# Four edits to the schedule of a Fourier mixing and maxout kernel: the order of the head, three split units, and when a copy is made

## The chip, the cores and the metric

The kernel runs on one core of a Trainium2 chip. The core has five instruction queues that run side by side: TensorE (PE in the profile; PEld is its loading of weights), VectorE (DVE), ScalarE (ACT), GpSimd (POOL) and SyncE (SP, which here only issues transfers). DVE, ACT and PE can read or write PSUM, where products are summed; POOL works in SBUF alone. Each engine takes its instructions strictly in the order in which the kernel wrote them, and waits at semaphores for the others. The metric is the time of one execution on the device in microseconds (us); lower is better.

## The reference

The input x is 8 batches of 3072 rows by 256 columns. Each batch goes through a Fourier transform over its rows and one over its columns, and the real part is kept. The result, 24576 rows of 256, then goes through a maxout layer with a width of 768:

```python
X = np.fft.fft(np.fft.fft(x, axis=1), axis=2).real
h = np.maximum(np.maximum(X @ w1, X @ w2), X @ w3)
out = h @ w_out
```

## The kernel before, in words

**Mixing.** The transform over rows is done in two stages of products with small tables, and its even and odd parts are kept apart in two bf16 tiles per batch, `tE` and `tO` (128 x 1536 each, class `Mix`). The transform over columns is never carried out on x: it is folded into the weights once, at the start (`products`, `keep`, `differ`, `prep_first`, `prep_second`; the results are `g_all`, `gd_all`, `gw`). Because sine and cosine are symmetric, the lower 64 partitions of x's tile `xt` are loaded, and the upper 64 are a mirrored copy of them: `mirror` (L129, and L133 for the first column) in batches 0 and 1, and from batch 2 on eight pieces (`turn`, L129 on ACT) and `mirror_first` (L138 on ACT). `xt` has two buffers, for even and odd batches.

**Units.** A batch has 18 units (3 blocks of 512 columns times 6 groups of 128 hidden features); g counts them over all batches. A unit makes the maximum of three products for a row (`hp`) and for its mirror row (`hm`). `begin` makes the first half and `finish` the second; the loop at the end writes begin(g), then finish(g-1). There are two forms:

- Not split (`unit_plus`, `unit_minus`, `unit_out`): the weights are taken relative to w1, so two sums remain, `pse2` and `pse3`. Four products of 512 columns make the first half (L484, L485) and two more (L491) turn it into the second; each half is taken by a Relu on ACT (`stmp`, L497) and a maximum on DVE (L498).
- Split (`third` and the branches in `begin` and `finish`): the third product is made apart and earlier, two units ahead. TensorE makes `e3` and `d3` (L856, L858), ACT scales `d3` into `odd3` (L860), DVE adds a rank-one term into `even3` (L861), and POOL makes their sum and difference (`plus3`, `minus3`, L865). Then `begin` needs two products (L875, L876) and one DVE instruction (L877), and `finish` one product (L491) and one DVE instruction (L889). A split unit has five products of 512 columns, another six.

`is_split` decides: odd units from g = 7 on are split; even ones by their place in the batch, in no unit of batch 0 and in the units 0, 4, 8, 12 and 14 of all others (`EXTRA`, `EXTRA_LAST`, which are the same).

**Second layer.** The products with `w_out` of one block of columns (L547, with L563 and L570) are pieces of a generator. `l2_some(10)` issues ten of them after each unit, so that TensorE has work while DVE, ACT and POOL finish a unit. DVE adds the linear part (L575), and the rows are stored by SP, or scattered by POOL (L651, `scatter`, units 0, 4, 8, 14 by `PACE`, and unit 16 in the last batch). The last block of the last batch has a form of its own (`l2_last`).

**Order.** The order is written out by hand, no scheduler changes it. `at(batch, unit, fn)` puts a function into a plan that is run after a unit's products: loads of a later batch's x (`load_x`, on POOL's queue, in units 13 and 18 three batches ahead), its mirrored copies (`turn`), and the mixing of the next batch (`ahead0`, `ahead`).

**Head.** Before unit 0 the mixing of batch 0 is done in a straight line: x comes in four pieces, each is mirrored by DVE, multiplied (`m.s`, L394), and evicted to `tb`; DVE transposes `tb` (L427); `k_first` (L696) makes the first 512 columns of `tE` and `tO`, in two halves of 256 each, evicted by DVE and ACT (L698). The fourth piece's first column is copied by POOL (L133). Three DVE instructions of one column (L220) make `sgn` and `dif`, after the transpose. PSUM has eight banks: in the head five belong to `ps_s` and three to `ps_f`; then `ps_s` is given up and its banks go to `ps_l1`, `ps_w3` and `ps_o`, in which the units sum.

Of the kernel before, what the change touches and what calls it, by code (L numbers as in the profile page):

```python
# [9 lines left out]
FP32 = mybir.dt.float32  # L10
# [4 lines left out]
ALU = mybir.AluOpType  # L15
# [13 lines left out]

FIRST_OF = (4, 8, 1)  # L30
PACE = (0, 4, 8, 14)
EXTRA, EXTRA_LAST = (0, 4, 8, 12, 14), (0, 4, 8, 12, 14)


def _parts(g):

    done = [(12 + i - 1, slice(128 * i + 96, 128 * i + 128)) for i in range(4)]
    for i in range(4 if g < 2 else 3):
        done.append((FIRST_OF[g] + i - 1, slice(128 * i, 128 * i + 96)))
    if g == 2:  # L40
        done += [(16, slice(384, 480, 2)), (15, slice(385, 480, 2))]
    return done
# [3 lines left out]
def kernel(  # L46
# [9 lines left out]
    nc = tc.nc  # L56

    B, S, D = x.shape
# [3 lines left out]
    TOKB = 512  # L62
    NHALF = 1536
    UNITS = 3 * NJC
# [8 lines left out]
    ps_f = ctx.enter_context(tc.tile_pool(name="ps_f", bufs=3, space=bass.MemoryType.PSUM))  # L73
# [30 lines left out]
    g_all = consts.tile([128, 4 * DFF], BF16, tag="g_all")  # L104
    g_all = g_all.rearrange("p (c k j) -> p c k j", k=4, j=128)
# [6 lines left out]
    sgn = consts.tile([128, 1], FP32, tag="sgn")  # L112
    wcol = consts.tile([128, NJC], FP32, tag="wcol")
    dif = consts.tile([128, 1], FP32, tag="dif")
    t_mid = consts.tile([128, 2, B], BF16, tag="t_mid")

    def load_x(b, s0, s1, h):

        rows = x[b].rearrange("(a s) d -> a s d", s=96)
        lo, hi = (s0, s1) if h == 0 else (max(s0, 1), min(s1, 48))  # L120
        src = rows[:, lo:hi, :] if h == 0 else rows[:, 97 - hi:97 - lo, :][:, ::-1, :]
        return nc.gpsimd.dma_start(out=xt[b % 2][32 * h:32 * h + 32, lo:hi, :], in_=src)  # L122

    def mirror(b, s0, s1):

        t = xt[b % 2]
        fn = (nc.vector.tensor_copy, (nc.gpsimd.tensor_copy, nc.vector.tensor_copy)[s0 >= 25],
              nc.scalar.copy)[min(b, 2)]
        fn(out=t[64:128, s0:s1, 1:128], in_=t[0:64, s0:s1, 255:128:-1])  # L129
        if b < 2:  # L130
            if b == 0:
                fn = nc.scalar.copy if s0 < 40 else nc.gpsimd.tensor_copy
            fn(out=t[64:128, s0:s1, 0], in_=t[0:64, s0:s1, 128])  # L133

    def mirror_first(b):

        t = xt[b % 2]
        nc.scalar.copy(out=t[64:128, :, 0], in_=t[0:64, :, 128])  # L138
# [3 lines left out]
    ps_s = ps_s_cm.__enter__()  # L142
# [7 lines left out]
    pidx = gen.tile([128, 1], FP32, tag="pidx")  # L150
# [56 lines left out]
    turn = gen.tile([128, 2], FP32, tag="turn")  # L207
# [10 lines left out]
    def scal(out, in0, s1, op0, s2=None, op1=None, eng=None):  # L218
        kw = {} if op1 is None else {"op1": op1}
        return (eng or nc.vector).tensor_scalar(out=out, in0=in0, scalar1=s1, scalar2=s2,  # L220
                                                op0=op0, **kw)
# [113 lines left out]
    def prep_first():  # L335

        for i in range(2):
            for half in range(2):
                psg = ps_f.tile([128, 512], FP32, name="psg", tag="ps")
                product(psg, 0, i, half, 384, 768)  # L340
                (nc.vector.tensor_copy, nc.scalar.copy)[half](
                    out=g_all[:, 3:6, 2 * i + half, :],
                    in_=psg[:, 0:384].rearrange("p (c j) -> p c j", j=128))
                if half:
                    differ(i, i + 1, 384, 768)
                yield
# [8 lines left out]
    def prep_second():  # L355

        for jp in range(NJC // 2):
            pst = ps_f.tile([128, 512], FP32, name="pst", tag="ps")
            for k in range(2):
                jc = jp * 2 + k  # L360
                for fc in range(2):
                    nc.tensor.matmul(
                        pst[:, k * 256:(k + 1) * 256],
                        w1_bf[:, fc * DFF + jc * 128: fc * DFF + jc * 128 + 128],
                        md[fc], start=(fc == 0), stop=(fc == 1))
            (nc.scalar.copy if jp == 2 else nc.vector.tensor_copy)(
                out=g1t[:, jp * 512:(jp + 1) * 512], in_=pst)
            yield
        psw = ps_f.tile([128, 512], FP32, name="psw", tag="ps")
        for half in range(2):  # L370
            for jc in range(NJC):
                nc.tensor.matmul(
                    psw[:, half * 256:(half + 1) * 256],
                    g1t[:, jc * 256 + half * 128: jc * 256 + half * 128 + 128],
                    wout_bf[:, jc * 256:(jc + 1) * 256],
                    start=(jc == 0), stop=(jc == NJC - 1))
        nc.vector.tensor_copy(out=gw[:, 0:512], in_=psw)
        nc.scalar.activation(out=gw[:, 512:768], in_=psw[:, 256:512], func=AX.Copy, scale=sgn)
        yield
# [96 lines left out]
                                 tab[:, NHALF:NHALF + 1], start=True, stop=True)  # L476
            nc.scalar.copy(out=t_mid[:, :, self.b], in_=ps3[:, 0:2])

    def unit_plus(te, to, jc, n, pool3, tag3):

        pse2 = ps_l1.tile([128, TOKB], FP32, name="pse2", tag="pse2")
        pse3 = pool3.tile([128, TOKB], FP32, name="pse3", tag=tag3)
        for (pse, i) in ((pse2, 0), (pse3, 1)):
            nc.tensor.matmul(pse[:, 0:n], g_all[:, jc, 2 * i, :], te, start=True, stop=False)  # L484
            nc.tensor.matmul(pse[:, 0:n], g_all[:, jc, 2 * i + 1, :], to, start=False, stop=True)  # L485
        return pse2, pse3

    def unit_minus(pses, to, jc):
# [177 lines left out]
    def warm_up(n):  # L666
        for _ in range(n):
            nc.tensor.matmul(warm, zero[:, 0:128], zero, start=True, stop=True)
# [10 lines left out]
    m.s(2, pool=ps_s)  # L679
    m.s(3, pool=ps_s)  # L680
    warm_up(1)
    mirror(0, *FIRST[3])
    m.s(4, pool=ps_s)
    warm_up(2)
# [4 lines left out]
    def k_first(which):  # L689

        for h in range(2):
            ps2 = ps_s.tile([128, 512], FP32, name="ps2", tag="ps")
            for (i, cols) in _parts(0):
                at = cols.start - 256 * h
                if 0 <= at < 256:
                    nc.tensor.matmul(ps2[:, at:at + cols.stop - cols.start], m.col(i, which),  # L696
                                     (te_tab, to_tab)[which][:, cols], start=True, stop=True)
            (dve, nc.scalar.copy)[h](out=(m.tE, m.tO)[which][:, 256 * h:256 * h + 256],  # L698
                                     in_=ps2[:, 0:256])

    m.s(6, pool=ps_s)
    m.t()
    scal(sgn, pidx, 0.0, ALU.is_equal)
    scal(sgn, sgn, 2.0, ALU.mult, -1.0, ALU.add)
    scal(dif, sgn, 1.0, ALU.subtract)
    warm_up(2)
    nc.scalar.activation(out=nmd_all, in_=vm, func=AX.Sin, scale=float(-2.0 * math.pi / 256.0),
                         bias=turn[:, 1:2])
# [46 lines left out]
    ps_w3 = ctx.enter_context(tc.tile_pool(name="ps_w3", bufs=1, space=bass.MemoryType.PSUM))  # L755
    ps_o = ctx.enter_context(tc.tile_pool(name="ps_o", bufs=2, space=bass.MemoryType.PSUM))
# [3 lines left out]
    first, second = prep_first(), prep_second()  # L760
# [10 lines left out]
    def at(b, unit, fn):  # L771
        plan.setdefault((b + unit // UNITS, unit % UNITS), []).append(fn)
# [27 lines left out]
    def turn(b, ch):  # L800
        mirror(b, *EIGHTHS[ch])
# [16 lines left out]
    for b in range(2, B):  # L818
        for h in range(2):
            if b > 2:  # L820
                at(b - 3, (13, 18)[h], lambda b=b, h=h: load_x(b, 0, NS, h))
        for ch in range(8):
            at(b - 2, 5 + ch + 3 * (b == 2), lambda b=b, ch=ch: turn(b, ch))
        at(b - 2, 13 + 3 * (b == 2), lambda b=b: mirror_first(b))

    ahead0 = {3: ("s0", "s1"), 4: ("s2", "y0"), 5: ("s3", "s4"), 6: ("s5", "s6", "y1", "u"),
              7: ("z0", "z1"), 12: ("x",), 13: ("kO0",), 14: ("v0", "kE0", "kO1"),
# [10 lines left out]

    def is_split(g):
        if g % 2 == 0:  # L840
            return (UNITS <= g < B * UNITS and
                    g % UNITS in (EXTRA if g < (B - 1) * UNITS else EXTRA_LAST))
        return 7 <= g < B * UNITS

    def operands(g):
# [21 lines left out]
    def begin(g, dst):  # L867

        te, to, _, jc = operands(g)
        if is_split(g):  # L870
            if g % 2:
                pse2 = ps_l1.tile([128, TOKB], FP32, name="pse2", tag="pse2")
            else:
                pse2 = ps_w3.tile([128, TOKB], FP32, name="pse3", tag="pse3")
            nc.tensor.matmul(pse2, g_all[:, jc, 0, :], te, start=True, stop=False)  # L875
            nc.tensor.matmul(pse2, g_all[:, jc, 1, :], to, start=False, stop=True)  # L876
            nc.vector.scalar_tensor_tensor(out=dst, in0=pse2, scalar=0.0, in1=sums[g][0],  # L877
                                           op0=ALU.max, op1=ALU.max)
            return (pse2,)
        pses = unit_plus(te, to, jc, TOKB, *((ps_o, "po") if g % 2 else (ps_w3, "pse3")))  # L880
        unit_out(pses, dst, TOKB)
        return pses

# [11 lines left out]
    for g in range(B * UNITS):  # L895
        b, u = divmod(g, UNITS)
        blk, jc = divmod(u, NJC)
# [14 lines left out]
        pses = begin(g, hp[:, jc, :])  # L912
# [53 lines left out]
```

## Time and profile before

| | before |
|---|---|
| median of 3 runs (lowest to highest) | 388.24 us (387.73 to 388.91) |
| the profiled execution, its own time | 388.26 us |
| its span in the profile | 386.5 us |
| busy in the span: PE, DVE, POOL, ACT | 369.5, 335.7, 331.7, 242.7 us |
| granted TensorE clock | 1.00 |

Mean durations of the instructions that the change touches, all 128x512:

| line | engine | what | ns |
|---|---|---|---|
| L865 | POOL | plus, minus | 1269, 1270 |
| L860 | ACT | odd | 597 |
| L861 | DVE | even | 737 |
| L877, L889 | DVE | hp, hm of a split unit | 687, 680 |
| L497 | ACT | stmp of a unit that is not split | 599 |
| L498 | DVE | hp, hm of a unit that is not split | 687 |
| L129 | ACT | one copy of x of 64x762 | 820 to 825 |

A profile is read in three steps. The busy times say which engine could be the bound. The chain that ended last says which instruction waited for which, back from the end. The order of time shows, for one stretch, each instruction with its start, its duration and, in brackets, how long its engine had stood still and what ended that. A matmul's duration contains its latency, so the distance between two starts is what TensorE really spends on it.

### The profile page before, as it was taken

What the parts mean: (1) busy time and instruction counts of PE and PEld (TensorE: products, weight loads), DVE (VectorE), ACT (ScalarE), POOL (GpSimd) and SP (SyncE); (2) the same over time, 40 slices, a digit from 0 to 9 for tenths busy, and PEclk for the clock granted to TensorE, in tenths of its full rate; (3) what the DMA queues carried; (4) which work ended last, traced back from release to release, by engine and by line L of the source; (5) the groups of instructions that cost most, each with busy time, mean ns of one, the idle gap of its engine ahead of it and who ended that gap; (6) DMA issues with size and microseconds to landing.
All of it is one profiled execution on the core that took longest, in us unless ns stands there. A gap on an engine that the chain in (4) does not pass through costs nothing.

```text
span 386.5 us, 7957 instructions
## 1 busy us (share of the span) xinstructions
PE 369.5 (96%) x2737; PEld 234.8 (61%) x2786; DVE 335.7 (87%) x566; ACT 242.7 (63%) x455; POOL 331.7 (86%) x355
## 2 busy tenths in 40 slices
PE   6699999999999999999999999999999999999994
PEld 2354566565665666656665666666665667666664
DVE  7798797789997998989987998989987998989982
ACT  6877789567756677567756777567856436434320
POOL 9994557968999899989999899989988899879991
PEclk9999999999999999999999999999999999999999
DMA  8999736695269735695269834695224633312217
GB/s 118 168 197 152 158 114 101 189 162 177 71 133 204 196 120 106 181 213 180 67 120 200 209 110 112 188 187 184 85 56 128 186 113 97 96 61 98 77 63 225
DMA packets 51299, 54.13 MB, mean 140 GB/s; under 512 B 25813, under 2 KB 44268, under 8 KB 50563
## 3 DMA queue, kind: packets, MB, share of 16 engines
q0 software_dynamic: 19392, 26.45, 33.3%
q1 hardware_dynamic: 31334, 26.57, 26.5%
q10 hardware_dynamic: 532, 0.59, 0.5%
q8 instruction: 22, 0.36, 0.4%
q14 instruction: 19, 0.16, 0.1%
HBM read 36.95 MB, written 30.81 MB: 175 GB/s over the span
## 4 chain that ended last, share of the span: by engine, by line
PE 81%; POOL 9%; DVE 4%; issue 3%; ACT 2%; DVEq 0%; POOLq 0%
PE po L547 29%; PE pse L491 9%; PE pse L876 5%; PE e L856 5%; PE d L858 5%; PE pse L875 5%; PE po L570 4%; PE pse L485 4%; PE pse L484 3%; PE ps L460 3%; POOL plus L865 3%; PE ps L394 3%; PE pl L563 2%; POOL minus L865 2%; POOL xt L122 1%
## 5 line engine op out<-in xcount | busy, mean ns | idle before, releaser
L865 POOL TENSOR_TENSOR plus<-even,odd 128x512 bf16<-128x512 f32 x104 | 132.0, 1269 | 38.5 <-DVE even L861 31.1
L865 POOL TENSOR_TENSOR minus<-even,odd 128x512 bf16<-128x512 f32 x104 | 132.1, 1270 | 0.0
L860 ACT ACTIVATE odd<-d 128x512 f32<-128x512 f32 x104 | 62.1, 597 | 63.8 <-PE d L858 50.3
L877 DVE SCALAR_TENSOR_TENSOR hp<-pse,plus 128x512 bf16<-128x512 f32 x104 | 71.4, 687 | 26.0 <-PE pse L876 21.5
L547 PE MATMUL po<-wout_bf,hp 128*128 128x256 bf16 x576 | 86.1, 273 | 0.0
L547 PE MATMUL po<-wout_bf,hm 128*128 128x256 bf16 x576 | 78.6, 273 | 0.0
L861 DVE SCALAR_TENSOR_TENSOR even<-vb,wcol,e 128x512 f32<-128x512 bf16 x104 | 76.6, 737 | 0.0
L547 PEld LDWEIGHTS <-hp 128*128 128x128 bf16 x576 | 56.3, 98 | 26.2
L889 DVE SCALAR_TENSOR_TENSOR hm<-pse,minus 128x512 bf16<-128x512 f32 x104 | 70.7, 680 | 0.8 <-PE pse L485 0.4
L547 PEld LDWEIGHTS <-hm 128*128 128x128 bf16 x576 | 56.3, 98 | 16.3
L491 PE MATMUL pse<-tO,gd_all 128*128 128x512 bf16 x183 | 63.2, 380 | 0.8 <-DVE hp L877 0.2
L497 ACT ACTIVATE stmp<-pse 128x512 bf16<-128x512 f32 x80 | 47.5, 599 | 19.0 <-PE pse L491 8.8
L129 ACT COPY xt<-xt 64x762 bf16<-64x762 bf16 (+1 forms) x48 | 39.8, 838 | 2.3 <-DMA xt<-in_x_dram 1.3
L575 DVE TENSOR_TENSOR kq<-po,even 128x512 f32<-128x512 f32 x60 | 40.9, 682 | 0.0
L856 PE MATMUL e<-tE,g_all 128*128 128x512 bf16 x104 | 39.4, 379 | 0.3
L858 PE MATMUL d<-tO,gd_all 128*128 128x512 bf16 x104 | 39.4, 379 | 0.0
L876 PE MATMUL pse<-tO,g_all 128*128 128x512 bf16 x94 | 35.6, 379 | 1.7 <-issue 1.0
L570 PE MATMUL po<-gw,tO 128*128 128x512 bf16 x92 | 34.9, 379 | 0.0
L498 DVE TENSOR_TENSOR hp<-pse,stmp 128x512 bf16<-128x512 f32 x40 | 27.5, 687 | 6.7 <-ACT stmp L497 3.6
L875 PE MATMUL pse<-tE,g_all 128*128 128x512 bf16 x84 | 31.9, 380 | 0.7 <-DVE hm L498 0.5
L567 ACT COPY even<-pl 128x512 f32<-128x512 f32 x46 | 26.8, 583 | 8.3 <-DVE kq L575 7.8
L498 DVE TENSOR_TENSOR hm<-pse,stmp 128x512 bf16<-128x512 f32 x40 | 27.5, 687 | 4.2 <-ACT stmp L497 3.0
(183 smaller groups left out, 485.4 us busy)
## 6 DMA issues: line engine op xcount, KB each, us to landing
db<-tb SPq DMA_DIRECT2D x21, 192.0 KB
xt<-in_x_dram POOLq DMA_DIRECT2D x5, 784.0 KB, 8.2
xt<-in_x_dram POOLq DMA_DIRECT2D x5, 752.0 KB, 8.7
out_dram<-obuf SPq DMA_DIRECT2D x8, 384.0 KB
out_dram<-kq SPq DMA_DIRECT2D x8, 384.0 KB
vb<-vd SPq DMA_DIRECT2D x23, 128.0 KB
out_dram<-kq SPq DMA_DIRECT2D x7, 288.0 KB
out_dram<-kq SPq DMA_DIRECT2D x15, 128.0 KB
```

Of the source, the lines that this page charges most:

```text
L491: nc.tensor.matmul(pse, gd_all[:, jc, i, :], to, start=False, stop=True, skip_group_check=True)
L498: nc.vector.tensor_tensor(out=dst, in0=src3, in1=stmp[:, 0:n], op=ALU.max)
L547: nc.tensor.matmul(po, hcols(jc), wout_bf[:, jc * 256:(jc + 1) * 256], start=False, stop=(jc == NJC - 1), skip_group_check=True)
L856: nc.tensor.matmul(e3, g_all[:, jc, 2, :], te, start=True, stop=True)
L858: nc.tensor.matmul(d3, gd_all[:, jc, 1, :], to, start=True, stop=True)
L860: nc.scalar.activation(out=odd3, in_=d3, func=AX.Copy, scale=-0.5)
L861: nc.vector.scalar_tensor_tensor(out=even3, in0=vb, scalar=wcol[:, jc:jc + 1], in1=e3, op0=ALU.mult, op1=ALU.add)
L865: nc.gpsimd.tensor_tensor(out=dst, in0=even3, in1=odd3, op=op)
L875: nc.tensor.matmul(pse2, g_all[:, jc, 0, :], te, start=True, stop=False)
L876: nc.tensor.matmul(pse2, g_all[:, jc, 1, :], to, start=False, stop=True)
L877: nc.vector.scalar_tensor_tensor(out=dst, in0=pse2, scalar=0.0, in1=sums[g][0], op0=ALU.max, op1=ALU.max)
L889: nc.vector.scalar_tensor_tensor(out=dst, in0=pses[0], scalar=0.0, in1=sums.pop(g)[1], op0=ALU.max, op1=ALU.max)
```

## The change

It has four parts.

1. In the head, the first column of the fourth piece of batch 0's x is copied by DVE, directly behind its mirror, and not by POOL; `sgn` and `dif` are made before that mirror; `k_first` takes its PSUM tiles for `tO` from `ps_f`; and unit 0 multiplies `tE` into both sums before it multiplies `tO`.
2. In batch 1, the eight copies of batch 3's x and the copy of its first column are placed in the units 6 to 13 and 14, and not 5 to 12 and 13.
3. In batch 0, the units 12 and 14 are split.
4. In the last batch, unit 14 is not split.

```diff
-EXTRA, EXTRA_LAST = (0, 4, 8, 12, 14), (0, 4, 8, 12, 14)
+EXTRA = (12, 14), (0, 4, 8, 12, 14), (0, 4, 8, 12)
...
             if b == 0:
-                fn = nc.scalar.copy if s0 < 40 else nc.gpsimd.tensor_copy
+                fn = nc.scalar.copy if s0 < 40 else nc.vector.tensor_copy
             fn(out=t[64:128, s0:s1, 0], in_=t[0:64, s0:s1, 128])
...
-    def unit_plus(te, to, jc, n, pool3, tag3):
+    def unit_plus(te, to, jc, n, pool3, tag3, first=False):
 
         pse2 = ps_l1.tile([128, TOKB], FP32, name="pse2", tag="pse2")
         pse3 = pool3.tile([128, TOKB], FP32, name="pse3", tag=tag3)
-        for (pse, i) in ((pse2, 0), (pse3, 1)):
-            nc.tensor.matmul(pse[:, 0:n], g_all[:, jc, 2 * i, :], te, start=True, stop=False)
-            nc.tensor.matmul(pse[:, 0:n], g_all[:, jc, 2 * i + 1, :], to, start=False, stop=True)
+        steps = [(pse2, 0, 0), (pse2, 0, 1), (pse3, 1, 0), (pse3, 1, 1)]
+        if first:
+            steps = steps[0::2] + steps[1::2]
+        for (pse, i, k) in steps:
+            nc.tensor.matmul(pse[:, 0:n], g_all[:, jc, 2 * i + k, :], (te, to)[k],
+                             start=(k == 0), stop=(k == 1))
         return pse2, pse3
...
     warm_up(1)
+    scal(sgn, pidx, 0.0, ALU.is_equal)
+    scal(sgn, sgn, 2.0, ALU.mult, -1.0, ALU.add)
+    scal(dif, sgn, 1.0, ALU.subtract)
     mirror(0, *FIRST[3])
...
-            ps2 = ps_s.tile([128, 512], FP32, name="ps2", tag="ps")
+            ps2 = (ps_s, ps_f)[which].tile([128, 512], FP32, name="ps2", tag="ps")
...
     m.t()
-    scal(sgn, pidx, 0.0, ALU.is_equal)
-    scal(sgn, sgn, 2.0, ALU.mult, -1.0, ALU.add)
-    scal(dif, sgn, 1.0, ALU.subtract)
     warm_up(2)
...
         for ch in range(8):
-            at(b - 2, 5 + ch + 3 * (b == 2), lambda b=b, ch=ch: turn(b, ch))
-        at(b - 2, 13 + 3 * (b == 2), lambda b=b: mirror_first(b))
+            at(b - 2, 5 + ch + 3 * (b == 2) + (b == 3), lambda b=b, ch=ch: turn(b, ch))
+        at(b - 2, 13 + 3 * (b == 2) + (b == 3), lambda b=b: mirror_first(b))
...
     def is_split(g):
         if g % 2 == 0:
-            return (UNITS <= g < B * UNITS and
-                    g % UNITS in (EXTRA if g < (B - 1) * UNITS else EXTRA_LAST))
+            return g < B * UNITS and g % UNITS in EXTRA[(g >= UNITS) + (g >= (B - 1) * UNITS)]
         return 7 <= g < B * UNITS
...
-        pses = unit_plus(te, to, jc, TOKB, *((ps_o, "po") if g % 2 else (ps_w3, "pse3")))
+        pses = unit_plus(te, to, jc, TOKB, *((ps_o, "po") if g % 2 else (ps_w3, "pse3")),
+                         first=(g == 0))
```

## The prediction

> **What bounds the kernel now.** I read the page's busy shares, then the chain that ended last, then the order of time around every place where that chain leaves TensorE or TensorE starts late.
>
> ```profile
> PE 369.5 (96%) x2737; PEld 234.8 (61%) x2786; DVE 335.7 (87%) x566; ACT 242.7 (63%) x455; POOL 331.7 (86%) x355
> ...
> PE 81%; POOL 9%; DVE 4%; issue 3%; ACT 2%; DVEq 0%; POOLq 0%
> ```
>
> TensorE is the bound; what counts is its work and the moments at which it starts late. At full rate 512-column products start 0.216 us apart (20.62, 20.84, 21.05) and 256-column ones 0.108, so a larger step between two starts is lost time. After 20 us I find four losses that the change touches.
>
> Order of time, head (start, duration, engine, line, operands, in brackets the idle time before and who ended it):
>
> ```profile
> 14.04 0.22 POOL L133 COPY xt<-xt 64x9 bf16<-64x9 bf16 x1
> 14.31 0.41 PE L394 MATMUL ps<-xt,tab 128*64 128x512 bf16 x2 [0.74 <-POOL xt L133]
> 15.55 3.77 DVE L427 STREAM_TRANSPOSE yb<-tb 128x2048 uint32<-128x2048 uint32 x1
> 19.86 0.37 ACT L698 CAST tE<-ps 128x256 bf16<-128x256 f32 x1 [0.19 <-PE ps L696]
> 20.20 0.37 ACT L698 CAST tO<-ps 128x256 bf16<-128x256 f32 x1
> 20.62 0.38 PE L484 MATMUL pse<-tE,g_all 128*128 128x512 bf16 x1 [0.46 <-ACT tO L698]
> ```
>
> TensorE's first stage waits for POOL's column copy; its first unit multiplies tE, but waits for tO. Batch 1, units 5 to 7:
>
> ```profile
> 84.82 0.82 ACT L129 COPY xt<-xt 64x762 bf16<-64x762 bf16 x1 [1.32 <-DMA xt<-in_x_dram]
> 87.26 0.82 ACT L129 COPY xt<-xt 64x762 bf16<-64x762 bf16 x1
> 88.11 0.60 ACT L497 ACTIVATE stmp<-pse 128x512 bf16<-128x512 f32 x1
> 88.74 0.69 DVE L498 TENSOR_TENSOR hm<-pse,stmp 128x512 bf16<-128x512 f32 x1 [0.49 <-ACT stmp L497]
> 89.48 0.38 PE L875 MATMUL pse<-tE,g_all 128*128 128x512 bf16 x1 [0.54 <-DVE hm L498]
> ```
>
> ACT stands at the first copy of batch 3's x until the load lands; stmp, hm and TensorE follow late. Last batch:
>
> ```profile
> 367.69 1.28 POOL L865 TENSOR_TENSOR plus<-even,odd 128x512 bf16<-128x512 f32 x1
> 369.01 0.69 DVE L877 SCALAR_TENSOR_TENSOR hp<-pse,plus 128x512 bf16<-128x512 f32 x1 [1.16 <-POOL plus L865]
> 369.75 0.38 PE L491 MATMUL pse<-tO,gd_all 128*128 128x512 bf16 x1 [0.25 <-DVE hp L877]
> ```
>
> From 347.9 POOL has no gap worth naming; at unit 15 DVE, then TensorE, wait for it.
>
> **The change, part by part.**
>
> *Column on DVE.* DVE's mirror (13.36, 0.65) ends at 14.01. The nearest row, DVE's L133 of 64x12, takes 0.18 and starts 0.07 before its predecessor ends: done at 14.12, TensorE at 14.17, a gain of 0.14. Ends: 0.06 as in the shortest DVE rows (gain 0.25), or held by a POOL instruction (below). Everything up to the transpose hangs on this product (L401 at 14.76, transpose at 15.55), so the 0.14 goes on. POOL loses 0.22 of work; the weight loads, x0u copies, x loads and yb copies queued behind start up to 0.18 earlier. The three sgn/dif instructions (3 x 0.15) move into DVE's 0.84 idle before 13.36, which ends on a load: nothing; without that gap 0.45 on the same path.
>
> *Products with tE first.* They now need only ACT's tE, ending at 20.23 instead of tO's 20.57; tO's two PSUM tiles come from the other pool, so the unit's banks don't wait for tO either. Start 20.28 for 20.62: 0.34. The third product, at 20.71, finds tO ready (20.57 + 0.05). The first sum of the unit ends only 0.13 earlier, so hp follows at about 22.5, but its reader starts at 23.43 - 0.48 = 22.95: covered by 0.45. From 20.62 to 28.6 TensorE starts are dense, and its small waits at 29 to 46 follow ACT and DVE work that TensorE itself started. Head: 0.14 + 0.34 = **0.48** (from 0, all absorbed there, to 0.59).
>
> *Units 12 and 14 of batch 0 split.* Six products become five: 2 x 0.216 = **0.43** less TensorE. ACT loses 2 x 599 and gains 597 ns per unit. DVE: 737 + 687 + 680 for 2 x 687, +0.73 each; POOL: +2.54 each. The gaps before:
>
> ```profile
> 53.45 1.27 POOL L865 TENSOR_TENSOR plus<-even,odd 128x512 bf16<-128x512 f32 x1 [2.05 <-DVE even L861]
> 55.79 0.69 DVE L877 SCALAR_TENSOR_TENSOR hp<-pse,plus 128x512 bf16<-128x512 f32 x1 [0.69 <-PE pse L876]
> 58.09 1.27 POOL L865 TENSOR_TENSOR plus<-even,odd 128x512 bf16<-128x512 f32 x1 [2.14 <-ACT xt L129]
> 61.16 0.69 DVE L877 SCALAR_TENSOR_TENSOR hp<-pse,plus 128x512 bf16<-128x512 f32 x1 [1.24 <-PE pse L876]
> ```
>
> POOL idles 2.05 + 2.14 here and 0.31 + 0.88 + 0.69 up to 66.67, in all 6.07 for 5.08; DVE 1.93 for 1.46. Queued behind on POOL are unit 13's and 15's sums, batch 3's first load (60.52) and a scatter (61.43). Placing the sums one after another from 51.45, unit 15's end at 61.4, so that load leaves 0.9 late; its second half, which decides, is issued at 72.82 after the gaps. Batch 1's units 11 to 15 run the same order of instructions with no late TensorE start but one of 0.09 at 98.61: I take no new wait. Ends: 0.43 gained, or DVE's 1.46 all exposed (1.03 lost).
>
> *Batch 3's copies a unit later.* The first copy moves behind unit 6's first stmp, odd and even, to where the second stands now (87.26, some 86.5 without the stall); the load landed at 84.75. The stall goes: 89.48 against 88.56 + 2 x 0.108 = 88.78, 0.70, plus 0.07 at 87.05: **0.77** (ends 0 and 0.77). Late next is the last copy and the first-column copy at units 13 and 14; behind them on ACT stand the evictions at 103.69 and 104.17, 0.93 later at most, with 1.21 of ACT idle following: nothing. No DMA moves with them.
>
> *Unit 14 of the last batch not split.* TensorE +0.216, ACT +0.6, DVE -0.73, POOL -2.54. Unit 15's plus ends 2.5 earlier, so three late starts go: 369.75 against 368.68 + 6 x 0.108 = 369.33 (0.42); 371.61 against 371.48 (0.13); 372.20 against 372.05 (0.15). 0.70 - 0.22 = **0.48** (ends -0.22 and 0.48). ACT idles over 3 us there, covering the added stmp.
>
> Sum: 0.48 + 0.43 + 0.77 + 0.48 = 2.16. The profiled execution took 388.26 (span 386.5 and 1.8 around it), 0.02 above the median: 388.26 - 2.16 = **386.1**.
>
> **The rivals.**
>
> 1. *The head's gain is absorbed* by the waits at 30 to 46 (TensorE idles 0.33 before 33.65 on ACT's tO). Against: those follow TensorE's own start. 386.6.
> 2. *The tail keeps its waits* because DVE, packed from 355 on, is late without POOL: +0.22 for -0.48, 386.8. Against: DVE's 1.16 gap ends on POOL.
> 3. *DVE becomes batch 0's bound*: its 1.46 is exposed, 386.1 + 1.46 = 387.6. For: the idle gaps end on TensorE and may not be movable. Against: batch 1's same units.
> 4. *POOL's backlog, slower.* If the gaps can't be used because even comes late, the 5.08 stand before batch 1, and from 66.67 to 78.9 POOL has no gap to lose them. Unit 1's plus ends at 70.40, 0.94 before its hp (71.34), so TensorE waits 5.08 - 0.94 = 4.1: 390.2. It decides from a backlog of 3.1 on. Against: 6.07 of gaps.
> 5. *DVE's column is held by POOL.* DVE's L332 of 128x384 took 1.44 beside a POOL copy (25.67) and 0.35 at 29.29; L129 of 64x2032 took 1.01 beside a POOL memset and 0.69 at 7.93, beside a weight-load issue. Behind one such issue (0.73 from 14.02) the column ends at 14.93, 0.62 lost for 0.14 gained: 386.9. Against: that row at 7.93.
> The Trainium skill, "SBUF — State Buffer", section "Who interferes with whom", says that VectorE and GpSimd share one port pair as an exclusive lock, taken by VectorE copies in the two-port mode, and that whoever issues first keeps it for the whole instruction. The 1.44 and 1.01 agree; by that rule with POOL first the result would be rival 5's, while the 7.93 row shows an issue that held nothing.
>
> **How the numbers follow.** Chances: forecast 0.48 (own range 385.7 to 386.5), 1 0.13, 2 0.12, 3 0.13, 4 0.07, 5 0.04; 0.03 for more, if the packed head also loses DVE's 1.44 (down to 385.3). About 0.3% (1.2 us, so 387.1 and 389.4) is what a measurement of this kernel can tell from no change. Faster: all but 3 and 4, 0.80; within: 3, 0.13; slower: 4, 0.07. The range 385.5 to 387.6 leaves out 4 and most of "more": 0.1.
>
> **What would show it.** First unit's product at about 20.14, its wait ended by tE; DVE's L133 at about 14; no ACT wait on the load near 84, and TensorE without the gap at 89; POOL near-gapless from 51 to 61 with hp not waiting on plus; no hp wait on POOL at unit 15 of the last batch; 104 split units become 105. Wrong would be: hp waits on POOL in batches 0 and 1, a new ACT wait on the load, or TensorE gaps at 30 to 46 grown by what the head won.

## The result and the profile after

| | before | after |
|---|---|---|
| median of 6 runs each (lowest to highest), us | 387.81 (387.65 to 388.91) | 386.01 (385.87 to 386.62) |
| ratio, 95% interval | 1 | 0.9952 (0.9939 to 0.9966) |
| the profiled execution, its own time, us | 388.26 | 386.05 |
| its span, us | 386.5 | 384.2 |
| granted TensorE clock | 1.00 | 0.999 |

The change makes the kernel faster by 0.48%; the forecast was 386.1. In a later comparison the same kernel gave 386.51 us (386.24 to 387.98, 6 runs) beside 388.56, a ratio of 0.9949 (0.9933 to 0.9965). One of the ten runs of the kernel without the move of the copies, below, took 486.57 us at a granted clock of 0.754, where all other runs had 0.989 to 1.000; it is left out of the medians and ratios.

The page of the changed kernel, busy shares and the chain that ended last by engine:

```profile
PE 372.2 (97%) x2785; PEld 234.6 (61%) x2785; DVE 336.9 (88%) x568; ACT 242.5 (63%) x454; POOL 334.3 (87%) x356
...
PE 90%; DVE 3%; DMA 2%; ACT 2%; issue 1%; POOL 1%; DVEq 0%; POOLq 0%
```

POOL's share of the chain falls from 9% to 1% and TensorE's rises from 81% to 90%, while POOL's own busy time rises by 2.6 us. (The TensorE busy times of the two pages aren't comparable: before's trace lacks some 50 matmul records, after's lacks none.)

The best way to see where the time went is to set the two traces beside each other product by product, and to read at a few places how much earlier TensorE starts the same work. I call this the lead. It is worked out from the order of time of both traces; by the forecast it should be 2.16 at the end.

| stretch | lead gained, us | what lies there |
|---|---|---|
| to 44 us | 0.16 | head |
| 44 to 66 | 0.43 | units 12 and 14 of batch 0, split |
| 66 to 81 | 0.00 | batch 1 up to the copies |
| 81 to the steady part behind 98 | 0.85 | copies of batch 3's x |
| from there to 346 | 0.00 | batches 2 on |
| last batch | 0.47 | its unit 14 not split |
| TensorE's last start | 1.91 | 379.40 for 381.32 |

The other 0.37 of the span's 2.28 comes behind TensorE's last start. From VectorE's last copy to the end of the span it is 4.42 us before and 4.05 after. Over all fourteen profiles of this document it is 4.20 to 4.72 (mean 4.42) in the six with unit 14 of the last batch split and 3.64 to 4.27 (mean 4.03) in the eight without. So it seems to go with that part of the change, to which the forecast gave nothing behind TensorE; by which path it does isn't shown, and two executions of one kernel can differ by 0.22 (4.05 and 4.27, the changed kernel).

Order of time of after, the head (start, duration, engine, line, operands, idle time before and who ended it):

```profile
13.12 0.90 DVE L129 COPY xt<-xt 64x1143 bf16<-64x1143 bf16 x1
13.37 0.28 POOL L145 IOTA kq<- 128x96 f32 x1
13.54 0.44 POOL L145 IOTA kq<- 128x1 f32 x1
13.63 0.77 POOL L184 DMA_DIRECT2D w_bf<-in_moe_w_dram  x1
13.94 0.47 DVE L133 COPY xt<-xt 64x9 bf16<-64x9 bf16 x1
14.46 0.41 PE L394 MATMUL ps<-xt,tab 128*64 128x512 bf16 x2 [0.90 <-DVE xt L133]
15.71 3.78 DVE L427 STREAM_TRANSPOSE yb<-tb 128x2048 uint32<-128x2048 uint32 x1
20.03 0.37 ACT L704 CAST tE<-ps 128x256 bf16<-128x256 f32 x1 [0.19 <-PE ps L702]
20.37 0.37 ACT L704 CAST tO<-ps 128x256 bf16<-128x256 f32 x1
20.45 0.59 PE L487 MATMUL pse<-tE,g_all 128*128 128x512 bf16 x2
```

VectorE's mirror takes 0.90 for 0.65, but only because it begins earlier: it ends at 14.02, as before (14.01). Its column copy takes 0.47 where the forecast had 0.18, so the product starts at 14.46, 0.15 later than before. The first unit starts at 20.45, right behind tE (20.40) and 0.29 ahead of the end of tO (20.74).

Order of time of after, batch 1, units 5 to 7, and the last batch, units 14 and 15:

```profile
83.99 0.60 ACT L500 ACTIVATE stmp<-pse 128x512 bf16<-128x512 f32 x1 [1.08 <-PE pse L487]
86.01 0.82 ACT L129 COPY xt<-xt 64x762 bf16<-64x762 bf16 x1
86.86 0.60 ACT L500 ACTIVATE stmp<-pse 128x512 bf16<-128x512 f32 x1
88.23 0.38 PE L877 MATMUL pse<-tE,g_all 128*128 128x512 bf16 x1
...
364.19 1.27 POOL L867 TENSOR_TENSOR plus<-even,odd 128x512 bf16<-128x512 f32 x1 [0.34 <-DVE even L863]
366.44 0.69 DVE L879 SCALAR_TENSOR_TENSOR hp<-pse,plus 128x512 bf16<-128x512 f32 x1 [0.60 <-PE pse L878]
368.71 1.27 POOL L867 TENSOR_TENSOR plus<-even,odd 128x512 bf16<-128x512 f32 x1 [0.79 <-DVE even L863]
```

The copy no longer stands in front of stmp and waits for nothing. In the last batch POOL has idle time again, and VectorE's hp of unit 15 waits for TensorE and not for POOL.

### The profile page after: what moved, and what is told of

Read it like the earlier page. It is cut to its first block, busy times and chain, and to the rows that moved or that the text cites. A ratio compares the mean times of both kernels' runs of the same rounds, so it can differ in the third digit from the quotient of the medians.

```text
span 384.2 us, 8003 instructions
## 1 busy us (share of the span) xinstructions
PE 372.2 (97%) x2785; PEld 234.6 (61%) x2785; DVE 336.9 (88%) x568; ACT 242.5 (63%) x454; POOL 334.3 (87%) x356
## 4 chain that ended last, share of the span: by engine, by line
PE 90%; DVE 3%; DMA 2%; ACT 2%; issue 1%; POOL 1%; DVEq 0%; POOLq 0%
PE po L550 32%; PE pse L494 10%; PE pse L487 8%; PE pse L877 6%; PE pse L878 6%; PE e L858 6%; PE d L860 6%; PE po L573 5%; PE ps L460 3%; PE ps L394 3%; PE pl L566 3%; DMA xt<-in_x_dram 2%; DVE yb L427 1%; ACT stmp L500 1%; PE psg L311 1%
## 5 line engine op out<-in xcount | busy, mean ns | idle before, releaser
L867 POOL TENSOR_TENSOR plus<-even,odd 128x512 bf16<-128x512 f32 x105 | 133.4, 1271 | 31.4 <-DVE even L863 25.8
L867 POOL TENSOR_TENSOR minus<-even,odd 128x512 bf16<-128x512 f32 x105 | 133.5, 1272 | 0.0
L879 DVE SCALAR_TENSOR_TENSOR hp<-pse,plus 128x512 bf16<-128x512 f32 x105 | 72.2, 687 | 25.0 <-PE pse L878 22.8
L863 DVE SCALAR_TENSOR_TENSOR even<-vb,wcol,e 128x512 f32<-128x512 bf16 x105 | 77.4, 737 | 0.0
L500 ACT ACTIVATE stmp<-pse 128x512 bf16<-128x512 f32 x78 | 46.3, 599 | 21.2 <-PE pse L487 10.3
L877 PE MATMUL pse<-tE,g_all 128*128 128x512 bf16 x105 | 39.9, 380 | 0.1
L878 PE MATMUL pse<-tO,g_all 128*128 128x512 bf16 x105 | 39.8, 379 | 0.0
L494 PEld LDWEIGHTS <-gd_all 128*128 128x128 bf16 x183 | 17.9, 98 | 20.3 <-issue 2.5
```

What stands on the lines that cost most here:

```text
L494: nc.tensor.matmul(pse, gd_all[:, jc, i, :], to, start=False, stop=True, skip_group_check=True)
L863: nc.vector.scalar_tensor_tensor(out=even3, in0=vb, scalar=wcol[:, jc:jc + 1], in1=e3, op0=ALU.mult, op1=ALU.add)
L867: nc.gpsimd.tensor_tensor(out=dst, in0=even3, in1=odd3, op=op)
```

## The experiments

### Each part by itself

Four kernels, each the kernel before with one part of the change.

```diff
 head alone (p1_head): the changed kernel with
-EXTRA = (12, 14), (0, 4, 8, 12, 14), (0, 4, 8, 12)
+EXTRA = (), (0, 4, 8, 12, 14), (0, 4, 8, 12, 14)
-... 5 + ch + 3 * (b == 2) + (b == 3) ...   13 + 3 * (b == 2) + (b == 3)
+... 5 + ch + 3 * (b == 2) ...              13 + 3 * (b == 2)
 batch 0's split alone (p2_split): the kernel before with the change's is_split and
+EXTRA = (12, 14), (0, 4, 8, 12, 14), (0, 4, 8, 12, 14)
 copies alone (p3_copies): the kernel before with
+... + (b == 3) in the two lines of the copies
 last batch alone (p4_last): the kernel before with the change's is_split and
+EXTRA = (), (0, 4, 8, 12, 14), (0, 4, 8, 12)
```

> The kernel before with the head's edits alone. Theory A (the four parts are independent, each is worth what TensorE's starts show between the two profiles): the first unit starts at 20.45 and TensorE stands 0.16 us earlier than before from the head to its last product. Theory B (the parts feed each other: the copies' gain is partly owed to an earlier head): the shift grows at 89, by 0.1 us or more, because ACT's wait for the load shrinks or grows with the head. Under A the wait near 84 stays at 1.3 us, less or more by 0.16.

> The kernel before with units 12 and 14 of batch 0 split, nothing else. Theory A: TensorE 0.43 us earlier from 66 us on, POOL without a gap between 51 and 61, no DVE wait on POOL's plus there. Theory B (this part delays batch 3's load, which then costs the copies more): the load's second half is issued up to 0.6 us later against TensorE's own progress, ACT's wait near 84 grows from 1.32 to 1.6 to 2.0 us, and the gain is gone again at 90.

> The kernel before with batch 3's copies a unit later, nothing else. Theory A: TensorE's late start at 89.48 goes but for the 0.11 us that the other batches show at the same place, 0.66 us, and the excess of 0.09 to 0.2 at 98.6 goes too, 0.75 to 0.85 in all, with no ACT wait on the load. Rival (the first copy merely waits at its new place): ACT waits there for the load again and the gain is under 0.3 us.

> The kernel before with unit 14 of the last batch not split, nothing else. Theory A: TensorE's last product starts 0.47 us earlier (0.70 of late starts gone, 0.22 of work more), and DVE does not wait for plus at unit 15. Beyond TensorE the end comes another 0.3 to 0.4 us earlier, if POOL's last two scatters, which are issued 2 us earlier, no longer lie under the last stores; the rival for that is that this 0.36 between the two profiles is the scatter of one execution, then the time from DVE's last copy to the end stays at 4.4 us.

Measured, one run each, 387.94 us for the kernel before beside them; the lead gained in each stretch from the traces:

| | time, us | head | 44 to 66 | 81 on | last batch | at the last start |
|---|---|---|---|---|---|---|
| head alone | 387.73 | 0.14 | 0.00 | 0.43 | 0.01 | 0.58 |
| split alone | 387.04 | 0.00 | 0.42 | 0.84 | 0.00 | 1.26 |
| copies alone | 387.97 | -0.75 | 0.00 | 0.85 | 0.00 | 0.08 |
| last batch alone | 386.83 | 0.01 | 0.00 | 0.17 | 0.47 | 0.65 |
| the whole change | | 0.16 | 0.43 | 0.85 | 0.47 | 1.91 |

Split, copies and last batch gain in their own stretch what they gain in the whole, and the head gains 0.14 and not the 0.48 of the forecast. Two entries aren't the edit's. The copies' kernel lost 0.75 in the head, which it doesn't touch: there a POOL memset ran beside a VectorE mirror at 10.2 us and took 1.03 where it took 0.59 before, so POOL's column copy came at 14.32 for 14.04 (0.28); the rest came in front of the transposed column, with ScalarE's x0s (L450) at 19.09 for 17.93; its cause stays open. And the column "81 on" moves in kernels that leave the copies where they were; that is the next question. With the last batch alone, VectorE's last copy is followed by 3.64 us and not by the 4.4 that the expectation named as the sign of mere scatter.

### The copies: place or landing

In the kernel with the split alone the wait at the copies was gone as well. Either the split makes batch 3's second load land earlier, so that the move of the copies is worth nothing beside it, or the load had come early in that one execution. The changed kernel without its move of the copies tells it apart:

```diff
-            at(b - 2, 5 + ch + 3 * (b == 2) + (b == 3), lambda b=b, ch=ch: turn(b, ch))
-        at(b - 2, 13 + 3 * (b == 2) + (b == 3), lambda b=b: mirror_first(b))
+            at(b - 2, 5 + ch + 3 * (b == 2), lambda b=b, ch=ch: turn(b, ch))
+        at(b - 2, 13 + 3 * (b == 2), lambda b=b: mirror_first(b))
```

> The changed kernel with batch 3's copies back in units 5 to 12 and 13. Theory A (the loss depends on when the load lands, not on the place of the copies alone): where the load lands after about 83, ACT waits for it and TensorE loses the wait less 0.5; landing at 84.2 as in the changed kernel would cost 0.7 to 0.9 us against it, landing at 82.4 as with the split alone would cost nothing. Theory B (splitting units 12 and 14 makes the load land early in itself): landing at 82 to 83 again, no ACT wait, and the copies' move is worth nothing beside the other parts. Timed: 386.6 to 386.9 under A, 386.0 under B.

Measured: 386.51 us (9 runs), a ratio of 0.9953 (0.9940 to 0.9967); the changed kernel beside it 386.51, 0.9949 (0.9933 to 0.9965). Timed, the two can't be told apart, and the time alone leaves both theories standing. The trace can tell: order of time of the kernel without the move,

```profile
84.14 0.82 ACT L129 COPY xt<-xt 64x762 bf16<-64x762 bf16 x1 [1.23 <-DMA xt<-in_x_dram]
...
88.06 0.69 DVE L501 TENSOR_TENSOR hm<-pse,stmp 128x512 bf16<-128x512 f32 x1 [0.50 <-ACT stmp L500]
...
88.81 0.38 PE L877 MATMUL pse<-tE,g_all 128*128 128x512 bf16 x1 [0.52 <-DVE hm L501]
```

and of the kernel with the split alone:

```profile
83.10 0.83 ACT L129 COPY xt<-xt 64x762 bf16<-64x762 bf16 x1
84.16 0.60 ACT L497 ACTIVATE stmp<-pse 128x512 bf16<-128x512 f32 x1 [0.23 <-PE pse L485]
...
88.40 0.38 PE L874 MATMUL pse<-tE,g_all 128*128 128x512 bf16 x1
```

The same load, issued between 72.2 and 72.8 us (TensorE's start holds all that a kernel had gained up to there, 0.43 with the split for example):

| | landed | ACT's wait at the first copy | TensorE at the gap |
|---|---|---|---|
| before | 84.75 | 1.32 | 89.48 |
| last batch alone | 84.57 | 1.15 | 89.30 |
| head alone | 84.36 | 1.07 | 89.09 |
| the change without the move | 84.06 | 1.23 | 88.81 |
| split alone | 82.37 | none | 88.40 |
| the whole change | 84.17 | none, the copy stands later | 88.23 |

With the split and without the move the load landed at 84.06 and ACT waited: the split is not what takes the wait away. The landing at 82.37 is the execution's own, 10.0 us behind its issue for 11.7 to 11.9 in the other rows and 11.2 to 12.5 in the remaining profiles, all but one of which have the split; why, I can't say. So the move takes off a wait whose size hangs on the load: 0.58 of lead here (1.44 with it, 0.86 without, in the steady part). In the whole change it shows as 0.66 at the gap (0.11 of late start left of 0.71, and 0.07 gone ahead of it) and 0.20 at 98.61, where before's small late start is gone too; the latter also goes in the kernels with head alone and without the move, so it isn't the move's.

### The head: who holds VectorE

The step on which my forecast of the head rested is the column's 0.18. In the trace of after it is 0.47. Two explanations: POOL holds VectorE, by its iotas (instructions that write index numbers, here four in a row up to 13.98) or by the issue of the first weight load (13.63 to 14.40), which now starts 0.55 earlier because POOL no longer waits for x; or the copies are slow for a reason of their own (rows just landed, the load's tail). Three edits of the changed kernel:

```diff
 POOL's copies of x0u, which wait for x, ahead of its weight loads (h_u_first)
+    m.u()
     for k in range(3):
         load_w(k, 384, 768)
-    m.u()
 the column on ScalarE (h_act_col)
-                fn = nc.scalar.copy if s0 < 40 else nc.vector.tensor_copy
+                fn = nc.scalar.copy
 the column back on POOL (h_pool_col)
-                fn = nc.scalar.copy if s0 < 40 else nc.vector.tensor_copy
+                fn = nc.scalar.copy if s0 < 40 else nc.gpsimd.tensor_copy
```

> The changed kernel with the copies into x0u written ahead of the three weight loads on POOL's queue, so that POOL waits for DVE's column before it issues them. Theory A (in the changed kernel POOL, which lost its own wait, issues the weight loads at 13.6 and holds DVE's mirror and column): mirror at most 0.65, column about 0.2 instead of 0.47, the product at 14.05 to 14.2 instead of 14.46, first unit at 20.05 to 20.2. Rival (the column of 9 single elements a row is slow on DVE by itself): column 0.4 to 0.5, product no earlier than 14.35. Timed, the first would be 0.3 us under the changed kernel, which is near what the rounds can tell.

> The changed kernel with the fourth piece's column on ACT, like the other three. Theory A: the column (0.23 to 0.26 on ACT) is done under DVE's mirror, so the product starts right behind the mirror; the mirror itself stays held by POOL's weight loads (0.8 to 0.9), product at 14.05 to 14.15, first unit 0.3 to 0.4 earlier than in the changed kernel. Rival (nothing was held, DVE is slow): mirror 0.65, product at 13.85.

> The changed kernel with the column back on POOL, the rest of the head as changed. Theory A: weight loads start again behind the column at about 14.2, mirror 0.65, product at 14.3, and the first unit at 20.28, so the column's move cost 0.15 to 0.17 us and the order of the products alone is worth 0.34. Rival (the product was late for another reason, the landing of x): product at 14.4 or later, first unit at 20.4.

Order of time with x0u ahead of the weight loads:

```profile
12.90 1.14 POOL L145 IOTA kq<- 128x288 f32 x4
13.46 0.62 DVE L129 COPY xt<-xt 64x1143 bf16<-64x1143 bf16 x1 [0.41 <-DMA xt<-in_x_dram]
14.01 0.17 DVE L133 COPY xt<-xt 64x9 bf16<-64x9 bf16 x1
14.22 0.41 PE L394 MATMUL ps<-xt,tab 128*64 128x512 bf16 x2 [0.69 <-DVE xt L133]
...
20.19 0.59 PE L487 MATMUL pse<-tE,g_all 128*128 128x512 bf16 x2
```

and with the column on ScalarE:

```profile
13.50 0.23 ACT L133 COPY xt<-xt 64x9 bf16<-64x9 bf16 x1 [0.40 <-DMA xt<-in_x_dram]
13.52 0.49 DVE L129 COPY xt<-xt 64x1143 bf16<-64x1143 bf16 x1 [0.36 <-DMA xt<-in_x_dram]
14.11 0.41 PE L394 MATMUL ps<-xt,tab 128*64 128x512 bf16 x2 [0.47 <-DVE xt L129]
...
20.09 0.59 PE L487 MATMUL pse<-tE,g_all 128*128 128x512 bf16 x2
```

In a second profile of the changed kernel x landed later. POOL had stood 0.65 for a transfer of x (until 10.14) and made its iotas 0.9 later, and the issue behind them came after the column:

```profile
13.74 0.41 POOL L145 IOTA kq<- 128x288 f32 x1
13.95 0.55 DVE L129 COPY xt<-xt 64x1143 bf16<-64x1143 bf16 x1
14.43 0.20 DVE L133 COPY xt<-xt 64x9 bf16<-64x9 bf16 x1
14.68 0.41 PE L394 MATMUL ps<-xt,tab 128*64 128x512 bf16 x2 [0.37 <-DVE xt L133]
14.80 0.73 POOL L184 DMA_DIRECT2D w_bf<-in_moe_w_dram  x1
```

All heads with the changed order (in us; "landed" is x's fourth piece, "POOL free" the end of its last iota, "issue" the end of the weight-load issue behind it; the product is given as its start and, in brackets, how far that lies behind the mirror's end). The last four rows have the head edited:

| | landed | POOL free | mirror ends | issue ends | column takes, ends | product | first unit |
|---|---|---|---|---|---|---|---|
| head alone | 12.90 | 14.00 | 14.03 | 14.42 | 0.47, 14.43 | 14.48 (0.45) | 20.48 |
| after | 13.03 | 13.98 | 14.02 | 14.40 | 0.47, 14.41 | 14.46 (0.45) | 20.45 |
| without the move | 13.29 | 13.98 | 14.01 | 14.40 | 0.47, 14.41 | 14.46 (0.45) | 20.46 |
| four units split | 13.45 | 14.28 | 14.31 | 14.70 | 0.47, 14.71 | 14.76 (0.45) | 20.76 |
| flips on ScalarE | 13.79 | 13.85 | 14.37 | 14.50 | 0.21, 14.51 | 14.56 (0.19) | 20.53 |
| after, second profile | 13.86 | 14.84 | 14.50 | later | 0.20, 14.62 | 14.68 (0.18) | 20.65 |
| x0u first | 13.37 | 14.05 | 14.08 | later | 0.17, 14.18 | 14.22 (0.14) | 20.19 |
| column on ScalarE | 13.43 | 13.98 | 14.01 | 14.40 | 0.23 (ACT) | 14.11 (0.10) | 20.09 |
| both repairs | 13.78 | 14.59 | 14.45 | later | 0.23 (ACT) | 14.55 (0.10) | 20.51 |
| column on POOL | 13.69 | 14.29 | 14.32 | later | 0.22 (POOL) | 14.62 (0.30) | 20.57 |

First the column. Beside an issue it ended 0.01 behind it in all five profiles, and took 0.47 in the four in which the mirror was done 0.39 ahead of the issue's end. With no issue beside it it took 0.17 and 0.20. The issue takes 0.77 beside the column and 0.73 alone, so it is the column that waits. That is not a slow copy but a held one, and of the two explanations the first stands.

Counted from the mirror's end, the product starts at 0.45 with the column on VectorE beside the issue, at 0.14 with the issue out of the way, and at 0.30 with the column on POOL, in this kernel as in before. So the column's move cost 0.15, which was expected, though with the column on POOL the product itself came at 14.62 and not at the expected 14.3: POOL's iotas began 0.30 later in that execution.

The mirror in front of it is another matter, and two expectations had it wrong: with the column on ScalarE it took 0.49 and not 0.8 to 0.9, and in the second profile of after it ended 0.34 ahead of POOL's last iota and not behind it. An iota and the mirror hold each other, one instruction at a time. In the nine of the ten heads in which the mirror began under an iota, it ended 0.35 to 0.36 behind the end of one of them: of the third in seven (13.66 and 14.02 in after), of the first in after's second profile (14.15 and 14.50), of the second with both repairs (14.10 and 14.45); what decides which, isn't shown. The iota behind that one waits in its turn: the fourth, of 128x1, takes 0.44 where it comes right behind the one that the mirror waited for, and 0.13 where the mirror is done. That the mirror ends 0.03 to 0.04 behind POOL's last iota in seven rows thus comes of that iota's waiting for the mirror.

One end is open. With the flips on ScalarE the issue began 0.16 ahead of the mirror (13.73 and 13.89), and the mirror took only 0.48; so an issue doesn't hold all that VectorE begins beside it, and what in it held the column no run here shows.

The times: x0u first 386.76 us (10 runs, 385.54 to 389.49), a ratio of 0.9961 (0.9938 to 0.9984); column on ScalarE 385.69 (6 runs), 0.9934 (0.9907 to 0.9962); column on POOL 386.28, one run; before 388.16 beside them. 0.3 us is below what these runs can tell, so that the head is mended is shown in the traces and not in the times.

### The tail: the unit's form or POOL's chain

The late starts of the last batch could go because unit 14 has no thirds (its form), or because POOL has less in a row. In this kernel unit 14 is split again, and the two reversed copies of the last block, 0.61 us each on POOL, are made by ScalarE:

```diff
-EXTRA = (12, 14), (0, 4, 8, 12, 14), (0, 4, 8, 12)
+EXTRA = (12, 14), (0, 4, 8, 12, 14), (0, 4, 8, 12, 14)
-                    nc.gpsimd.tensor_copy(fl, t[:, 3 * TOKB - 1: 2 * TOKB - 1: -1])
+                    nc.scalar.copy(out=fl, in_=t[:, 3 * TOKB - 1: 2 * TOKB - 1: -1])
```

> The changed kernel with unit 14 of the last batch split again, but the two reversed copies of tE and tO (1.2 us of POOL at 364) moved to ACT. Theory A (the tail waited for POOL's chain, whatever is taken out of it): POOL's chain is 1.2 us shorter than before, DVE waits for unit 15's plus 0 to 0.2 us instead of 1.16, TensorE has 0.22 us less work than in the changed kernel, so its last product starts 0.05 to 0.22 earlier than there. Rival (it was the unit's form that freed DVE: 0.73 us of DVE work less): DVE stays late by 0.5 us or more and TensorE's end is later than in the changed kernel by 0.2 or more.

Measured: 386.33 us (10 runs, 386.09 to 386.8), 0.9948 (0.9932 to 0.9964). Order of time:

```profile
365.29 1.28 POOL L867 TENSOR_TENSOR plus<-even,odd 128x512 bf16<-128x512 f32 x1
366.60 0.69 DVE L879 SCALAR_TENSOR_TENSOR hp<-pse,plus 128x512 bf16<-128x512 f32 x1 [0.20 <-POOL plus L867]
```

hp still follows POOL's plus, but with 0.20 of idle time and not 1.16, and TensorE loses nothing by it. The lead gained in the last batch is 0.69, more than the 0.47 of the change by about the 0.22 of the one product that a split unit saves. So the unit's form need not change for the wait to go: 1.2 us less on POOL in a row did as much as 2.5 less.

### Batch 0: how much can POOL take?

If the idle time of POOL is what carries the two split units, four should overrun it.

```diff
-EXTRA = (12, 14), (0, 4, 8, 12, 14), (0, 4, 8, 12)
+EXTRA = (8, 10, 12, 14), (0, 4, 8, 12, 14), (0, 4, 8, 12)
```

> The changed kernel with units 8 and 10 of batch 0 split as well, 2.54 us more of POOL each. Theory A (POOL's gaps carry the split, and no more than they hold): before 51 POOL has gaps of some 0.9 and 1.6 us for 5.1 of work, so it is about 2.5 late from there; plus of units 11 to 15 ends only 0.8 to 1.7 before its use, so DVE waits on POOL and TensorE stands 1.0 to 1.5 us later than in the changed kernel at 66, 0.43 of saved work included. Rival (TensorE's work decides, POOL is no bound in batch 0): 0.43 us earlier at 66 than in the changed kernel, no DVE wait on plus.

Measured: 388.21 us, one run (the changed kernel 386.51 beside it). At 66 us TensorE is 2.0 later than in after, 0.3 of it from its head. POOL in order of time, of after and then of this kernel, from the first split unit of batch 0 to the load behind the last:

```profile
41.28 1.27 POOL L867 TENSOR_TENSOR plus<-even,odd 128x512 bf16<-128x512 f32 x1 [5.99 <-DVE even L863]
44.67 1.27 POOL L867 TENSOR_TENSOR plus<-even,odd 128x512 bf16<-128x512 f32 x1 [0.91 <-DVE even L863]
48.74 1.27 POOL L867 TENSOR_TENSOR plus<-even,odd 128x512 bf16<-128x512 f32 x1 [1.58 <-DVE even L863]
51.33 1.27 POOL L867 TENSOR_TENSOR plus<-even,odd 128x512 bf16<-128x512 f32 x1
...
61.15 0.61 POOL L122 DMA_DIRECT2D xt<-in_x_dram  x1
```

```profile
41.58 1.27 POOL L867 TENSOR_TENSOR plus<-even,odd 128x512 bf16<-128x512 f32 x1 [8.37 <-ACT odd L862]
44.04 1.26 POOL L867 TENSOR_TENSOR plus<-even,odd 128x512 bf16<-128x512 f32 x1
...
63.66 0.61 POOL L122 DMA_DIRECT2D xt<-in_x_dram  x1
```

In after POOL has idle time up to 48.74 and works without a gap from 51.33; with four units it works without a gap through nine units, from 41.58 to 63.66. That much was expected. But TensorE's late starts are mostly not there. Two of them, 0.80 and 0.85, lie ahead of the chain, where the thirds of units 7 and 8 are now made one behind the other and the second waits for ACT to take the first out of PSUM:

```profile
40.49 0.38 PE L860 MATMUL d<-tO,gd_all 128*128 128x512 bf16 x1 [0.63 <-ACT odd L862]
41.55 0.38 PE L566 MATMUL pl<-gw,tE 128*128 128x256 bf16 x2 [0.69 <-ACT odd L862]
...
54.65 0.38 PE L877 MATMUL pse<-tE,g_all 128*128 128x512 bf16 x1 [0.29 <-DVE hm L892]
58.21 0.38 PE L860 MATMUL d<-tO,gd_all 128*128 128x512 bf16 x1 [0.32 <-ACT yb L450]
```

Within the gapless stretch only 0.46 (54.65) and 0.48 (58.21) are late, the first of them behind hm, the second behind ACT. So four units lose, but 1.65 by crowding at one place on TensorE and ACT, and 0.94 in the stretch in which POOL is full. The expectation had 1.0 to 1.5 later by way of waits on POOL; it came out larger and mostly by another way. How much of the 0.94 is POOL's isn't settled: no wait in it ends on POOL by name.

### A version with both repairs

ScalarE makes the column and the reversed copies, and the last batch's unit 14 is split again (the edits of "column on ScalarE" and "flips on ScalarE" together).

> The changed kernel with the fourth piece's column on ACT, unit 14 of the last batch split again, and the reversed copies of tE and tO on ACT. Theory A (the two gains add): TensorE's last product 0.35 us earlier from the head and 0.22 from the tail, 378.8 to 378.9 for the changed kernel's 379.4; timed 0.4 to 0.6 us under the changed kernel, 385.4 to 385.7. Rival (the head's gain is the scatter of one execution's landing of x): 379.1 to 379.2 and 385.8.

> The changed kernel itself, beside the others on the same chip. Theory A of the parts: between the kernel before and the one with column and reversed copies on ACT, ratio to before 0.995 to 0.996. Its second profile also shows which of the head's numbers repeat: if POOL holds DVE, the fourth piece's mirror ends within 0.05 us of POOL's last iota or later, and the column within 0.05 of the end of POOL's first weight-load issue, whenever it starts under one. Rival: the column takes 0.47 again with no issue beside it.

Measured on the same chip: 385.99 us (385.77 to 386.62, 5 runs), 0.9929 (0.9916 to 0.9942), for the changed kernel 386.51, 0.9949 (0.9933 to 0.9965). The intervals overlap a little, so faster than before is shown, faster than the changed kernel is likely. In the profiles x landed alike (13.78 and 13.86); the first unit starts at 20.51 for 20.65 and TensorE's last product at 379.38 for 379.60. That is 0.22 earlier where 0.57 was expected: the tail gives its 0.22, but of the head's 0.14 almost nothing is left from 36 us on (0.02). The 0.35 expected of the head was the difference to an execution with the issue beside the column, and in the second profile of after it wasn't beside it.

## Why the prediction was right, and where it wasn't

**Bound, and three of the four parts.** TensorE's late starts were the right thing to count: its last start moves by 1.91, gained at the four places named, with 0.00 between them. Rival 1 didn't come, as the head's lead is 0.17 at 21 us and still 0.16 at 44; nor did rival 2, the tail's waits.

**Split in batch 0.** 0.43 forecast, 0.43 and, alone, 0.42. POOL is near-gapless from 51.33 to 61.15 as expected, and the load behind it was issued at 61.15 for 60.52, 0.63 late where 0.9 was reckoned. Rivals 3 (VectorE) and 4 (POOL's backlog) didn't come; in the four-unit kernel the larger loss comes from the order in which thirds are made, which neither rival had.

**Copies.** 0.77 forecast, 0.85 in that stretch. At the gap it is 0.66, and 0.11 of late start stays there, which I had reckoned as gained. The 0.20 at 98.61, which I had read as 0.09 and left in place, goes as well, but not by this edit. The term is a property of the executions as much as of the kernel: with the load at 84.06 it was 0.58, at 82.37 nothing.

**Tail.** 0.48 forecast, 0.47 and, alone, 0.47. The reason given, POOL's chain, is the one that the reversed copies on ScalarE confirm. What this part may bring behind TensorE's last start (means of 4.42 and 4.03 us) the prediction didn't have.

**tE first.** 0.34 forecast, and 20.45 against 20.40 for tE and 20.74 for tO gives the same.

**The column: the step that failed.** "Done at 14.12, TensorE at 14.17, a gain of 0.14" became 14.41 and 14.46, a loss of 0.15. I took the duration from a row with nothing of POOL beside it, though I had seen that POOL would start its weight loads earlier, and had set rival 5 at 0.04. Its mechanism is what happened, at a smaller price: 0.29 between forecast and product, where the rival had 0.76, since the column waits only for what is left of an issue that began at 13.63 and not for a whole one.

The Trainium skill, "SBUF — State Buffer", section "Who interferes with whom", has that rule: VectorE's two-port copies and GpSimd share one port pair, and who comes first holds it for the whole instruction. The mirror and the iotas (0.35 behind the end of one, and the next held in its turn) and the two orders of memset and mirror below agree with it. The issues agree in part: the column was held by one, but the mirror of 0.48 that began 0.16 behind an issue, and the one of 0.69 at 7.93 that the prediction had set against the rule, were not. That it is the port, and not something else that the two engines share, no run here shows.

**Luck in the total.** The forecast of 2.16 came near the 2.21 between the two profiled executions because the copies' stretch (+0.08) and what came behind TensorE's last start (0.37) made up for the 0.32 that the head missed. And 386.1 met the median of 386.01 though the medians differ by only 1.80: the one of before, 388.24 of three runs when the forecast was made, is 387.81 of six. The right total is therefore better than its parts.

## What to carry to other kernels

When work is taken from an engine, look at what its queue starts earlier for that, and beside whose work it then runs: here POOL, freed of a wait for x, issued its weight loads 0.55 us earlier and held the very copy that had been taken from it. Price a moved instruction from a row that has the same neighbour on the other engine, not from the shortest row of its kind. And where a wait ends on a transfer, price its removal as a range over executions (landings from 82.4 to 84.8 us in the table here), even when one profile shows it to a hundredth.

## What the runs showed of the hardware

- A VectorE copy of 64x9 single elements took 0.17 alone and up to 0.47 beside POOL's issue of a weight load, and ended 0.01 us behind that issue in five profiles. An issue of a DMA on POOL can thus hold VectorE; but a mirror of 64x1143 that began 0.16 behind one took 0.48, as short as any.
- A mirror of 64x1143 that began under POOL's iotas took 0.49 to 0.90 and ended 0.35 to 0.36 behind the end of one of them. In return it held the next: a 128x1 iota took 0.44 beside it and 0.13 alone.
- Between a memset and a mirror it goes by who comes first. In the profile of before POOL's memset of tb began at 10.16 and took 0.59, and VectorE's mirror of 64x2032, begun at 10.29, took 1.01; in that of the kernel with the copies alone the mirror began first, at 10.04, and took 0.69, and the memset, begun at 10.15, took 1.03. Which of the two it is hangs on the landing of x.
- The fourth piece of x landed between 12.90 and 13.86 us in executions whose loads were issued alike. The changed kernel's own two profiles have the first unit at 20.45 and 20.65: a scatter of 0.2 us, about what the edits of the head are worth.
